# A fused Fourier filter and MLP: at least two MLP steps between one batch's spectrum units, and batch 1's units spread over more steps

## The chip, the core and the metric

The kernel runs on one core of a Trainium2 chip. TensorE (PE) multiplies matrices, loading weights (PEld) beside its matmuls; VectorE (DVE), ScalarE (ACT) and GpSimd (POOL) do elementwise work; SyncE (SP) and POOL queue DMA transfers. Matmuls write to PSUM, from which DVE and ACT evacuate to SBUF. The metric is the device time of one execution in microseconds, the median of several runs.

## The reference

Eight sequences of 3008 tokens with 256 channels are filtered in the frequency domain, and every token then goes through an MLP.

```python
X = np.fft.rfft(x, axis=1)                    # x: 8 x 3008 x 256
F = (filt_r + 1j * filt_i)[None, :, :]
y = np.fft.irfft(X * F, n=x.shape[1], axis=1)
h = y.reshape(24064, 256) @ w_in              # w_in: 256 x 2048
g = h * (1.0 / (1.0 + np.exp(-beta * h)))     # beta: one per hidden unit
out = g @ w_out                               # w_out: 2048 x 256
```

## The kernel before

The transform of length 3008 = 47 x 64 is done with small matrices in four stages. For each batch: stage 1 (`s1`, 16 units) multiplies x by a table of cosines and sines, stages 2 and 3 (`s23`, 15 units, the "spectrum units") multiply by a second table, by the filter, and by the inverse of the second table, and stage 4 (`s4`, 16 units) multiplies by the inverse of the first. Between the stages the data are turned round through scratch tiles in DRAM: `s1` stores to `d1` (line 621), `a2_read` loads from it (line 628), `s23` stores to `d2` (line 669), `zz_read` loads from it (line 676). Stage 4 leaves `y`, the MLP's input.

The MLP runs over 47 blocks of 512 tokens and, in each, over 16 slices of 128 hidden units: 752 **steps**. A step s emits two matmuls that make `hps` (line 825, 512 columns each), the ScalarE activation that makes `gT` of it (line 834), then whatever transform units the plan has for this step, and then four matmuls of 256 columns (line 867) that add step s - 2's `gT` into the block's output `acc`. In a block's first slice only two of these four are emitted, and six in the next one. At a block's last slice the two halves of `acc` are copied to `ost` (both on DVE, but one half on ACT in blocks 0 to 5) and stored (lines 786 to 800). That falls in steps with s mod 16 = 1.

Batch 0's transform is done ahead of the first step, up to some units that are planned as `uz`. The transform of batch b > 0 is laid between the MLP steps of batch b - 1, by a **plan** that is written out by hand: `plan[s]` is a list of units that step s emits, in order. `place(a, z, units, clear, per)` spreads a list evenly from step a to step z; a step takes at most `per` units, counting those already there, and the next free one is used where it is full; with `clear` a unit that falls in the first two or last two steps of a block is moved on to the third of the next. A batch b from 2 on starts at step a = `first_step[b - 1]` (80, 176, 272, ...): its spectrum units are spread from a + 3 to a + 47, `zz_read` is in a + 53, the next batch's `s1` from a + 48 to a + 61, and `s4` from a + 63 to a + 78. Batch 1 has its own numbers, because it shares steps 0 to 79 with the rest of batch 0.

A spectrum unit i of `s23` works on two of 24 frequencies, and emits in this order:

- two matmuls of 256 columns into `ps2` (line 638; traces show tiles without their number, so `ps`),
- three DVE operations that read `ps2`: `p_t` (line 649) and two halves of `q_t` (lines 650 and 653),
- one POOL addition that makes `v_t` (line 654),
- from i = 3 on, two matmuls of 256 columns with the `v_t` of unit i - 3 into `ps3` (line 664), and an ACT evacuation of it to `z` (line 107, called at 667). Units 12, 13 and 14 have this last part alone. Every third unit is followed by a store of `z` to `d2`.

All PSUM tiles of the transform (`ps1`, `ps2`, `ps3`, `ps4`, `pz`) share one pool of three buffers, `fpsum`. Which of the three a tile gets is decided when the program is built, and a tile's first matmul waits for the reader of the tile that had the buffer before. `hps` has two buffers and `acc` three. Each engine runs its instructions in order, so a matmul that waits holds up everything behind it on PE. SP's queue is in order too, and holds all stores and all DMAs between the stages; x is loaded from POOL's queue.

Of the kernel before, what the change touches and what calls it, by code (L numbers as in the profile page):

```python
# [37 lines left out]
def kernel(  # L38
# [450 lines left out]
    for i in range(NK // 2 + FLAG):  # L489
# [6 lines left out]
        if i in TAB:  # L496
            n = TAB.index(i)
# [101 lines left out]
    def start(b):  # L599
        d1 = dpool.tile([J, KP, D], BF16, name="d1", tag="d1")  # L600
        d2 = dpool.tile([J, KP, D], BF16, name="d2", tag="d2")
        st[b] = {
            "x": xs.pop(b),
            "d1r": d1.rearrange("j r d -> r j d"),
            "d2r": d2.rearrange("j r d -> r j d"),
            "d1c": d1.rearrange("j (a k) d -> (j a) k d", a=4),
            "d2c": d2.rearrange("j (a k) d -> (j a) k d", a=4),
        }

    def s1(b, i, on_act):  # L610
        s = st[b]
        g, jj = divmod(2 * i, JG)
        if jj == 0:
            s["a1"] = apool.tile([KP, JG, D], BF16, name="a1", tag="a1")
        ps = fpsum.tile([P, 512], F32, name="ps1", tag="f")
        nc.tensor.matmul(  # L616
            ps[:KP], lhsT=t1[:], rhs=s["x"][:, 2 * i : 2 * i + 2, :], start=True, stop=True
        )
        evac(s["a1"][:, jj : jj + 2, :], ps[:KP], on_act)
        if jj + 2 == JG:  # L620
            nc.sync.dma_start(s["d1r"][:, g * JG : (g + 1) * JG, :], s["a1"][:])

    def a2_read(b):
        s = st[b]
        s["a2"] = []
        for h in range(NG):
            t = a2pool.tile([P, KG, D], BF16, name="a2", tag="a2")
            nc.sync.dma_start(t[:], s["d1c"][:, h * KG : (h + 1) * KG, :])
            s["a2"].append(t)
# [41 lines left out]
    def zz_read(b):  # L671
        s = st[b]
        s["zz"] = []
        for h in range(NJG):
            t = zzpool.tile([KP, JG, D], BF16, name="zz", tag="zz")
            nc.sync.dma_start(t[:], s["d2r"][:, h * JG : (h + 1) * JG, :])
            s["zz"].append(t)
# [12 lines left out]

    plan = {}

    def place(a, z, units, clear=False, per=1):
        last_at = a
        for n, go in enumerate(units):
            at = a + (z - a) * n / max(1, len(units) - 1)
            at = max(int(at), last_at)
            if clear and (at % NFB < 2 or at % NFB > 13):
                at += (2 - at) % NFB
            while len(plan.get(at, ())) >= per:  # L700
                at += 1
            plan.setdefault(at, []).append(go)
            last_at = at
        return last_at

    def u1(b, act=False):
        def unit(i):
            def go():
                if i == 0:
                    start(b)  # L710
                s1(b, i, act and i % 2 == 1)

            return go

        return [unit(i) for i in range(J // 2)]

    def u23(b):
        return [lambda i=i: s23(b, i) for i in range(NK // 2 + VLAG)]

    def u4(b, act=False):  # L720
        return [lambda i=i: s4(b, i, act and i % 2 == 1) for i in range(J // 2)]

    def uz(g, act=False):
        return [lambda i=i: turn_z(g, i) for i in range(2)] + [
            lambda i=i: last_z(g, i, act) for i in range(2 * NDC)
        ]

    def uf(a, z):
        return [
            go  # L730
            for k0 in range(a, z, JG)
            for at in (0, M)
            for go in load_filter(frr, filt_r, at, k0, JG, nc.sync)
        ]


    def ut(n):
        return [
            lambda k=k: nc.vector.tensor_scalar_mul(
                t3[M:P, k : k + NK // n], t3b[M:P, k : k + NK // n], -1.0  # L740
            )
            for k in range(0, NK, NK // n)
        ]

    def ux(b):
        def go():
            xs[b] = load_x(b, X_WHOLE)

        return [go]

    place(2, 14, uz(1, True))
    place(15, 29, uz(2))
    units = uz(3, True)
    place(20, 24, units[:2], per=2)
    place(34, 58, units[2:])

    first_step = [(S * b // TB) * NFB for b in range(B + 1)]
    if B > 1:
        units = u1(1, True)
        place(3, 8, units[: J // 4], per=2)  # L760
        place(10, 10, uf(0, JG), per=9)
        at = place(9, 14, units[J // 4 :], per=9)
        place(at + 1, at + 1, [lambda: a2_read(1)] + uf(JG, NK), per=9)
        place(14, 20, ut(4), per=2)
        at = place(25, 56, u23(1), per=2)
        assert at < 60
        place(60, 60, [lambda: zz_read(1)], per=9)
        place(67, 79, u4(1), per=2)
    if B > 2:
        place(36, 36, ux(2), per=9)  # L770
        at = place(50, 66, u1(2, True), per=3)
        assert at < 74
        place(74, 74, [lambda: a2_read(2)], per=9)
    for b in range(2, B):
        a = first_step[b - 1]
        place(a + 3, a + 47, u23(b), True)
        place(a + 53, a + 53, [lambda b=b: zz_read(b)], per=9)
        if b + 1 < B:
            place(a + 6 if b == 2 else a - 8, NBLK * NFB, ux(b + 1), per=9)
            place(a + 48, a + 61, u1(b + 1))  # L780
            place(a + 68, a + 68, [lambda b=b: a2_read(b + 1)], per=9)
        place(a + 63, a + 78, u4(b))
# [29 lines left out]
    for s in range(len(steps) + LAG):  # L812
        if s < len(steps):
# [5 lines left out]
            while pos < t0 + tn:  # L819
                b, n0 = divmod(pos, S)  # L820
# [20 lines left out]
        if s >= LAG:  # L841
# [16 lines left out]
            per = acc[0].shape[1]  # L858
# [55 lines left out]
```

## Time and profile before

| | us |
|---|---|
| median of 3 runs | 785.22 (784.85 to 785.43) |
| the profiled execution's own time | 785.37 |
| its span, first to last instruction | 783.3 |
| PE busy | 768.8 |
| ACT busy | 594.4 |
| DVE busy | 393.3 |
| POOL busy | 144.4 |

The profile shows one execution, with times from the span's start. Ends of matmuls are modelled, their starts are not, so the pace of TensorE is read from starts. Step 0's first matmul is at 36.2 us. The granted TensorE clock is full speed in all slices. A number after "x" counts merged instructions, and square brackets give the idle time of an engine before an instruction and what ended it.

### The profile page before, as it was taken

What the parts mean: (1) busy time and instruction counts of PE and PEld (TensorE: products, weight loads), DVE (VectorE), ACT (ScalarE), POOL (GpSimd) and SP (SyncE); (2) the same over time, 40 slices, a digit from 0 to 9 for tenths busy, and PEclk for the clock granted to TensorE, in tenths of its full rate; (3) what the DMA queues carried; (4) which work ended last, traced back from release to release, by engine and by line L of the source; (5) the groups of instructions that cost most, each with busy time, mean ns of one, the idle gap of its engine ahead of it and who ended that gap; (6) DMA issues with size and microseconds to landing.
All of it is one profiled execution on the core that took longest, in us unless ns stands there. A gap on an engine that the chain in (4) does not pass through costs nothing.

```text
span 783.3 us, 15454 instructions
## 1 busy us (share of the span) xinstructions
PE 768.8 (98%) x6015; PEld 547.8 (70%) x6111; DVE 393.3 (50%) x645; ACT 594.4 (76%) x922; POOL 144.4 (18%) x143
## 2 busy tenths in 40 slices
PE   8899999999999999999999999999999999999997
PEld 5767667666776667866668666786667766776665
DVE  7848836646446563474635746267452761500101
ACT  6987887886678867787677876778767788677776
POOL 8522501320013100231002310024000330000000
PEclk9999999999999999999999999999999999999999
DMA  9979764517801186022850238412371114100101
GB/s 190 253 174 228 176 191 132 128 67 202 221 28 68 68 209 194 28 81 94 197 167 28 95 111 183 149 64 81 108 209 40 64 68 128 49 34 28 55 28 54
DMA packets 84185, 91.46 MB, mean 117 GB/s; under 512 B 4498, under 2 KB 74276, under 8 KB 83154
## 3 DMA queue, kind: packets, MB, share of 16 engines
q1 hardware_dynamic: 81008, 73.95, 30.8%
q0 software_dynamic: 2816, 16.26, 10.7%
q8 instruction: 48, 0.79, 0.4%
q10 hardware_dynamic: 288, 0.26, 0.1%
q14 instruction: 25, 0.20, 0.1%
HBM read 57.16 MB, written 46.66 MB: 133 GB/s over the span
## 4 chain that ended last, share of the span: by engine, by line
PE 96%; ACT 1%; issue 1%; DMA 1%; DVE 1%; POOL 0%; DVEq 0%; POOLq 0%
PE acc L867 43%; PE hps L825 39%; PE ps L616 3%; PE ps L541 3%; PE ps L664 3%; PE ps L638 2%; DMA xg<-in_x_dram 1%; PE psz L461 1%; PE pz L533 0%; PE psa L325 0%; ACT a L107 0%; DVE q_t L653 0%; DVE q_t L650 0%; PE pt L351 0%; PE ps L435 0%
## 5 line engine op out<-in xcount | busy, mean ns | idle before, releaser
L834 ACT ACTIVATE gT<-hps,beta_sb 128x512 bf16<-128x512 f32 x752 | 515.6, 687 | 176.5 <-PE hps L825 155.4
L867 PE MATMUL acc<-wout_sb,gT 128*128 128x256 bf16 x3008 | 451.4, 272 | 2.7
L825 PE MATMUL hps<-y,win_sb 128*128 128x512 bf16 (+8 forms) x1636 | 427.6, 350 | 0.4 <-ACT gT L834 0.3
L867 PEld LDWEIGHTS <-gT 128*128 128x128 bf16 x3008 | 285.6, 98 | 127.6 <-ACT gT L834 0.2
L825 PEld LDWEIGHTS <-win_sb 128*128 128x128 bf16 x1730 | 165.0, 98 | 24.7 <-issue 0.6
L654 POOL TENSOR_TENSOR v_t<-p_t,q_t 128x512 bf16<-128x512 f32 x84 | 106.6, 1269 | 390.4 <-DVE q_t L653 327.6
L109 DVE COPY ost<-acc 128x512 f32<-128x512 f32 (+1 forms) x88 | 56.2, 677 | 192.6 <-PE acc L867 189.6
L109 DVE CAST a<-ps 96x512 bf16<-96x512 f32 x96 | 65.9, 686 | 87.3 <-PE ps L616 86.8
L111 DVE TENSOR_SCALAR y<-ps 128x376 bf16<-128x376 f32 (+1 forms) x119 | 63.9, 544 | 61.3 <-PE ps L541 61.2
L649 DVE TENSOR_TENSOR p_t<-ps,frr 128x512 f32<-128x512 f32 x84 | 58.1, 692 | 31.3 <-PE ps L638 28.9
L653 DVE TENSOR_TENSOR q_t<-ps,fri 64x512 f32<-64x512 f32 x84 | 58.2, 693 | 1.2
L650 DVE SCALAR_TENSOR_TENSOR q_t<-ps,fri 64x512 f32<-64x512 f32 x84 | 57.4, 684 | 1.1
L541 PEld LDWEIGHTS <-zz 96*128 96x128 bf16 x512 | 35.3, 97 | 29.3 <-issue 0.5
L107 ACT ACTIVATE z<-ps 128x512 bf16<-128x512 f32 x84 | 49.5, 589 | 0.0
L616 PE MATMUL ps<-xg,t 94*96 94x512 bf16 x112 | 42.1, 381 | 0.7
L541 PE MATMUL ps<-t,zz 96*128 96x94 bf16 x448 | 36.7, 205 | 1.1
L664 PE MATMUL ps<-v_t,t 128*128 128x256 bf16 x168 | 32.2, 274 | 0.8 <-DVE q_t L653 0.3
L638 PE MATMUL ps<-a,t 128*128 128x256 bf16 x168 | 32.1, 273 | 0.4
L118 POOL DMA_DIRECT2D xg<-in_x_dram x22 | 12.1, 552 | 101.7 <-PE acc L867 97.6
L638 PEld LDWEIGHTS <-t 128*128 128x128 bf16 x168 | 15.8, 98 | 14.6
L664 PEld LDWEIGHTS <-t 128*128 128x128 bf16 x168 | 15.3, 98 | 10.8 <-ACT z L107 3.8
L616 PEld LDWEIGHTS <-t 94*96 94x96 bf16 x112 | 13.6, 123 | 11.8
(120 smaller groups left out, 195.0 us busy)
## 6 DMA issues: line engine op xcount, KB each, us to landing
out_dram<-ost SPq DMA_DIRECT2D x80, 256.0 KB, 2.1
d<-a SPq DMA_DIRECT2D x28, 384.0 KB, 3.4
a<-d SPq DMA_DIRECT2D x28, 384.0 KB, 4.4
d<-z SPq DMA_DIRECT2D x28, 384.0 KB, 2.3
zz<-d SPq DMA_DIRECT2D x28, 384.0 KB, 6.8
xg<-in_x_dram POOLq DMA_DIRECT2D x6, 1280.0 KB, 10.0
frr<-in_filt_r_dram SPq DMA_DIRECT2D x12, 256.0 KB, 7.5
out_dram<-ost SPq DMA_DIRECT2D x18, 128.0 KB, 2.5
```

What stands on the lines that cost most here:

```text
L109: nc.vector.tensor_copy(dst, src)
L111: nc.vector.tensor_scalar_mul(dst, src, scale)
L541: nc.tensor.matmul(ps[:, e, :NP], lhsT=zz[:, jj + e, dc * P : (dc + 1) * P], rhs=tab[:], start=True, stop=True,)
L616: nc.tensor.matmul(ps[:KP], lhsT=t1[:], rhs=s["x"][:, 2 * i : 2 * i + 2, :], start=True, stop=True)
L638: nc.tensor.matmul(ps[:, e, :], lhsT=t2[:, k0 + e, 3:5, :].rearrange("p c k -> p (c k)"), rhs=s["a2"][g][:, kk + e, :], start=True, stop=True,
L649: nc.vector.tensor_tensor(p_t[:], ps[:], frr[:, ks_, :], ALU.mult)
L653: nc.vector.tensor_tensor(q_t[:M], ps[M:P], fri[M:P, ks_, :], ALU.mult)
L654: nc.gpsimd.tensor_tensor(v_t[:], p_t[:], q_t[:], ALU.add)
L664: nc.tensor.matmul(ps[:, e, :], lhsT=t3[:, k0 + e, :], rhs=v_t[:, e, :], start=True, stop=True)
L825: nc.tensor.matmul(hps[:, pos - t0 : pos - t0 + ln], lhsT=win_sb[:, dc, fb * P : (fb + 1) * P], rhs=ys[b][:, dc, n0 : n0 + ln], start=(dc ...
L834: nc.scalar.activation(gT[:, :tn], hps[:, :tn], ACT.Silu, scale=beta_sb[:, fb : fb + 1])
L867: nc.tensor.matmul(acc[tb // per][:, tb % per, :], lhsT=g_[:, tb * P : (tb + 1) * P], rhs=wout_sb[:, f_, :], start=(f_ == 0 and tb % per = ...
```

## The change

`place` gets an argument `gap`: a unit is put at least `gap` steps behind the one before it of the same list. The spectrum units of all batches are placed with a gap of 2. Batch 1's are spread from step 25 to 58 instead of 56, the first stage of batch 2 from step 54 to 68 instead of 50 to 66, and batch 2's `a2_read` is in step 75 instead of 74.

```diff
-    def place(a, z, units, clear=False, per=1):
+    def place(a, z, units, clear=False, per=1, gap=0):
         last_at = a
         for n, go in enumerate(units):
             at = a + (z - a) * n / max(1, len(units) - 1)
-            at = max(int(at), last_at)
+            at = max(int(at), last_at + gap if n else last_at)
             if clear and (at % NFB < 2 or at % NFB > 13):
                 at += (2 - at) % NFB
             while len(plan.get(at, ())) >= per:
...
-        at = place(25, 56, u23(1), per=2)
+        at = place(25, 58, u23(1), per=2, gap=2)
         assert at < 60
         place(60, 60, [lambda: zz_read(1)], per=9)
         place(67, 79, u4(1), per=2)
     if B > 2:
         place(36, 36, ux(2), per=9)
-        at = place(50, 66, u1(2, True), per=3)
-        assert at < 74
-        place(74, 74, [lambda: a2_read(2)], per=9)
+        at = place(54, 68, u1(2, True), per=3)
+        assert at < 75
+        place(75, 75, [lambda: a2_read(2)], per=9)
     for b in range(2, B):
         a = first_step[b - 1]
-        place(a + 3, a + 47, u23(b), True)
+        place(a + 3, a + 47, u23(b), True, gap=2)
```

Worked through the plan, the spectrum units stand in these steps (for batches 2 to 7 counted from a):

```
batch 1 before  25 27 29 31 33 36 38 40 42 44 47 49 51 53 56
batch 1 after   25 27 29 32 34 36 39 41 43 46 48 50 53 55 58
batch b before   3  6  9 12 18 19 21 25 28 34 35 37 40 43 50
batch b after    3  6  9 12 18 20 22 25 28 34 36 38 40 43 50
```

Batch 2's 16 units of stage 1 move from steps 50 to 66 to steps 54 to 68: before, the last was in step 66; after, the last three are in 66, 67 and 68, the latter two behind units of batch 1's stage 4. Units of the other lists stay in their steps.

## Prediction

> **What bounds the kernel now.** I read the page's busy shares and chain first, then the waits, then the timeline at each wait of TensorE.
>
> ```profile
> PE 768.8 (98%) x6015; PEld 547.8 (70%) x6111; DVE 393.3 (50%) x645; ACT 594.4 (76%) x922; POOL 144.4 (18%) x143
> ...
> PE 96%; ACT 1%; issue 1%; DMA 1%; DVE 1%; POOL 0%; DVEq 0%; POOLq 0%
> ```
>
> TensorE (PE) is the bound: it holds 96% of the chain. Nothing that another engine gains counts unless PE waits less. So I looked for PE's own waits, weight loads included, in the waits:
>
> ```profile
> PEld L664 <- ACT z L107: 3.8, 12, 0.5
> ...
> PEld L664 <- DVE q_t L653: 1.2, 2, 0.6
> ...
> PE ps L541 <- DVE q_t L653: 0.5, 1, 0.5
> ```
>
> The columns are total us, times, longest. Twelve times the second pair of matmuls in a spectrum unit (L664) waited for ScalarE's evacuation of `z`: two for each of batches 2 to 7. The other three are in batch 1. The total of 3.8 counts the weight load's idle time, part of which lies beside the matmul before it, so I take what PE lost from starts. On this trace's PE timeline a 512-column matmul is 0.217 us after the one before, a 256-column one 0.109; a plain step is 2 x 0.217 + 4 x 0.109 = 0.87 us, a spectrum unit 4 x 0.109 = 0.436, a stage-1 unit 0.217, a stage-4 unit 0.165. What a start is late against this is lost. One such place, batch 3, timeline:
>
> ```profile
> 239.02 0.38 PE L638 MATMUL ps<-a,t 128*128 128x256 bf16 x2
> ...
> 239.86 0.59 ACT L107 ACTIVATE z<-ps 128x512 bf16<-128x512 f32 x1
> 239.89 0.69 DVE L649 TENSOR_TENSOR p_t<-ps,frr 128x512 f32<-128x512 f32 x1
> ...
> 240.10 0.38 PE L638 MATMUL ps<-a,t 128*128 128x256 bf16 x2
> ...
> 240.50 0.11 PEld L664 LDWEIGHTS <-t 128*128 128x128 bf16 x2 [0.30 <-ACT z L107]
> 240.51 0.39 PE L664 MATMUL ps<-v_t,t 128*128 128x256 bf16 x2
> ...
> 241.29 0.69 DVE L653 TENSOR_TENSOR q_t<-ps,fri 64x512 f32<-64x512 f32 x1
> ```
>
> Unit 4 (239.02) is in step a+18, unit 5 (240.10) in a+19. Unit 5's L664 should start 0.22 after its L638, at 240.32, and starts at 240.51: 0.18 us lost. In the built program its PSUM tile has the buffer of unit 4's `ps3`, and ACT had started on that at 239.86 and was done at 240.45, because `gT` of the same step goes first. Units 9 and 10 (a+34, a+35) do the same. Going through all gaps: 0.38 + 0.18 in batch 2 (in the first an `ost` copy on ACT is in the way too), 0.18 + 0.18 in each of batches 3 to 7. **That is 0.57 + 5 x 0.37 = 2.41 us.** Batch 1 lost 0.43 at 75.34 (step 34), 0.42 at 84.58 (step 42) and 0.29 at 94.40 (step 51), 1.14 us in all, each behind DVE's `q_t` (L653).
>
> **The change part by part.** It adds and removes no instruction; it moves them, and the loss goes where a wait is no longer late.
>
> *Batches 2 to 7.* Unit 5 goes from a+19 to a+20, 6 from a+21 to a+22, 10 from a+35 to a+36, 11 from a+37 to a+38. Unit 5's L664 would start 0.87 later than it should now, at 240.32 + 0.87 = 241.19; z of unit 4 ends at 240.45, so 0.74 us are to spare (in batch 2, where it ended 0.38 late, still 0.5). What is late next? DVE's three operations take 0.69 + 0.68 + 0.69, with gaps 2.12 us a unit, against 2 x 0.87 + 0.436 = 2.18 us for two steps with a unit: it keeps up, barely. Unit 4's last ends at 241.98 and unit 6's L638, which waits for it, comes at 240.97 + 2.18 = 243.15: 1.2 to spare. DVE is behind here (unit 5 starts at 242.01, when unit 4 is done), so units 5 and 6 end when they end now, and POOL's `v_t` with them; unit 7 and later stay put. Units 9 to 12 are two steps apart where 11 and 12 were three; unit 12's matmuls wait for unit 10's `q_t`, which ends 5.1 us after unit 9's L638, and they come after about 6.5. The store of `z` behind units 5 and 11 moves 0.9 us later on SP; the one that `zz_read` waits for is behind unit 14, which stays. Saved: all 2.41 us.
>
> *Batch 1.* Unit 3 goes to step 32, 4 to 34. The built program has unit 4's L664 wait for unit 3's `q_t`. DVE is still busy with unit 2 until 73.17 whether unit 3 comes in step 31 or 32, so unit 3's `q_t` ends at 73.19 + 2.10 = 75.29. Without a unit in step 31, L638 of unit 4 comes at 74.65 and L664 at 74.87: 0.47 lost, in place of the 0.43 there now. Where a unit's L664 waits for the `q_t` of the unit two steps before (steps 43 and 50, each with a stage-4 unit between), it comes 2.18 + 0.165 + 0.218 = 2.56 after that unit's L638, and `q_t` is done after 0.22 + 0.27 (matmul end to DVE, as from 154.32 to 154.81 in batch 2) + 2.12 + 0.05 = 2.66: 0.1 each. The three-step gaps ahead (36 to 39, 43 to 46) let DVE catch up, which is why the 0.42 and 0.29 shrink to this.
>
> *Batch 2's stage 1.* Units 13, 14, 15 now fall in steps 66 to 68, beside stage 4. Unit 14's matmul waits for ACT's evacuation of unit 13. From the end of `hps` in step 66 its natural start is 0.217 + 0.218 (a block's first slice has half of L867) + 0.434 + 2 x 0.165 = 1.20. ACT starts `gT` after 0.26 to 0.3, the evacuation 0.58 behind that, and this takes 0.59, then 0.06: 1.5 to 1.6. Lost: 0.34, new. Moving `a2_read` costs nothing: its loads wait for the last `d1` store, which waits on SP behind eight output stores (4.49 us of issuing from 112.20 before), as it does now; they started at 120.09 with their first use at 129.11, 9 us cover against a landing of 5.2. If that cover went, each us beyond would be a us of PE at step 83.
>
> Batch 1 after: 0.47 + 0.1 + 0.1 + 0.34 = 1.0 against 1.14. **Sum: 2.41 + 0.15 = 2.6 us less**, 785.37 - 2.6 = 782.8 for the profiled execution, which is 0.15 above the median of the runs: 782.6.
>
> *A rule that speaks against the change.* Step 58 now has `gT`, a stage-4 evacuation, unit 14's `z` and a stage-1 evacuation on ACT, and 53, 55, 60 have two or three. The row first:
>
> ```profile
> 94.49 0.72 ACT L834 ACTIVATE gT<-hps,beta_sb 128x512 bf16<-128x512 f32 x1
> 95.06 0.64 ACT L107 ACTIVATE z<-ps 128x512 bf16<-128x512 f32 x1
> 95.53 0.62 ACT L107 ACTIVATE a<-ps 96x512 bf16<-96x512 f32 x1
> ```
>
> Starts lie 0.57 and 0.47 apart, closer than the durations: they overlap. The Trainium skill, "ScalarE: Activation LUTs", section "Rules for kernel authors", budgets about 0.3 us per activation and 0.83 ns per element, 0.725 us for 512. By the row, steps 58 to 60 hold 0.58 + 0.38 + 2 x 0.48, 0.58 and 0.58 + 0.48 = 3.6 us of ACT against 3.65 of PE (1.47 + 1.09 + 1.09): no loss. By the rule it is 2.8 + 0.7 + 1.45 = 4.95, 1.3 over; `hps` with two buffers lends 0.44, so 0.9 would be lost, and some 0.5 more at step 67: a saving of 1.2. I take the row, as the engine itself shows it; the rule's end stays in the range.
>
> **The rivals.**
>
> *DVE takes over the wait.* At two steps it has 0.06 us spare, and one `ost` copy is 0.68. If in batches 2 to 7 the 12 places keep 0.1 each as in batch 1, 1.2 of 2.41 is lost: 783.8. For it: batch 1's waits are all DVE's. Against it: there the buffers in question hang on ACT's `z`, as the waits show. Bound: 12 x 0.18, nothing gained, 785.0.
>
> *ACT piles up*, as the rule has it: 784.0.
>
> *Slower: batch 1's `zz_read` comes too late for step 67.* Unit 14 moves from step 56 to 58, stage 4 stays in 67. Before:
>
> ```profile
> 102.02 0.34 SPq L669 DMA_DIRECT2D d<-z  x1
> ...
> 104.36 3.63 SPq L676 DMA_DIRECT2D zz<-d  x4
> ```
>
> L664 of unit 14 was at 100.56, the store at 102.02, the reads at 104.36, and by the semaphore's updates in the trace the first read was in at 109.02, 4.66 later; PE needed it at 112.48. After, the store comes 1.7 behind L664 (ACT has one more ahead), the first read is in at 1.7 + 2.3 + 4.7 = 8.7; step 67's first use comes after 0.22 + 0.22 + 0.44 + 8 x 0.87 + 8 x 0.217 - 0.22 + 0.43 = 9.8. So 1.1 us to spare, 3.5 now. A read that took the slowest landing of these reads anywhere, 7.9, would stop PE for 2.1: 784.7. The time gets worse than before from a landing of 4.66 + 1.1 + 2.6 = 8.4 us; at 10.4 it would be 787.2. Against it: none took that long, and stores stand behind these reads on SP, not ahead.
>
> *The change doesn't do what it says:* the order of instructions shows units 5, 6, 10 and 11 moved in every batch, so only a different choice of buffers could keep the waits, and the built program has none in batches 2 to 7 on a reader less than two steps old. Then 785.2.
>
> **How the numbers follow.** About 0.2% (1.6 us) is what a measurement of this kernel can tell from no change: faster is below 783.65. The forecast, 782.6 with 782.0 to 783.3 for its own terms (0.3 for what batch 1 keeps or sheds, 0.3 between runs), has 0.78. DVE 0.08 and ACT 0.08 lie around 783.8 and 784.0, a third of each faster; late reads 0.04, of which 0.03 slower; no effect 0.02. Faster 0.78 + 0.05 = 0.83, slower 0.03, the rest 0.14. The range 781.8 to 784.2 takes in DVE's and ACT's cases and leaves out the late reads.
>
> **What would show it.** In the profile after, `PEld L664 <- ACT z` should be down from 12 times to at most one; unit 5 of batch 3 should start L664 0.22 behind its L638. Around 75 us an L664 should wait about 0.5 for `q_t`, and near 111 an L616 about 0.3 for ACT's `a`. An L541 waiting for a DMA there means the reads are late; `hps` waiting for `gT` between 95 and 105 means ACT piles up; L664 or L638 waiting for `q_t` in batches 2 to 7 means DVE. A time above 784.2 would make the forecast wrong, and so would a gain with the twelve waits still there.

## The result, and the profile after

The changed kernel takes 783.06 us, the median of 6 runs (782.44 to 783.57), against 785.04 (784.7 to 785.71) for the kernel before in the same measurement: a ratio of 0.9973 with a 95% interval of 0.996 to 0.9986. It is faster by 0.27%.

On the page after, the first lines of busy time and of the chain hardly differ from before:

```profile
span 781.3 us, 15549 instructions
...
PE 771.6 (99%) x6111; PEld 548.4 (70%) x6111; DVE 392.9 (50%) x645; ACT 594.3 (76%) x922; POOL 144.3 (18%) x143
...
PE 95%; DVE 2%; ACT 1%; DMA 1%; issue 0%; POOL 0%; DVEq 0%; POOLq 0%
```

PE's busy time even grows, as 96 matmul records are missing from the trace before (6015 against 6111). Busy time is no measure here. The waits show what changed (total us, times, longest):

```profile
PEld L664 <- DVE q_t L653: 1.4, 3, 0.6
...
DVE ost L109 <- DMA out_dram<-ost: 1.1, 1, 1.1
...
PE ps L664 <- DVE q_t L653: 0.7, 2, 0.4
```

The line `PEld L664 <- ACT z L107`, twelve times before, is gone. What is left of L664's waits are three in batch 1, all for DVE, and there is a line that was not there before: a copy of `ost` on DVE waited 1.1 us for an output store to land. Batch 3's units 4 and 5 in the timeline after:

```profile
238.95 0.38 PE L638 MATMUL ps<-a,t 128*128 128x256 bf16 x2
...
239.80 0.59 ACT L107 ACTIVATE z<-ps 128x512 bf16<-128x512 f32 x1
...
241.13 0.38 PE L638 MATMUL ps<-a,t 128*128 128x256 bf16 x2
...
241.34 0.38 PE L664 MATMUL ps<-v_t,t 128*128 128x256 bf16 x2
```

ACT's `z` of unit 4 is done at 239.80 + 0.59 = 240.39, and unit 5's L664 starts at 241.34, 0.21 behind its L638, as two 256-column matmuls take. Nothing is lost, and 0.95 us would have been to spare. (The prediction worked out 0.74: it took step a+19 as 0.87 us long, but that is a block's second slice, with six matmuls of L867 in place of four, 1.09 us.)

To compare kernels by their profiles I use the stretch from the first to the last matmul of `hps`, because what lies ahead of it is the same code and varied between executions. Before, then after (the view of the tile `hps`; min/median/max ns, then first and last start in us):

```profile
L825 PE MATMUL hps<-y,win_sb x1636: 192/379/380, 36.2 to 777.6; 128*128 128x512 bf16 x132, 128*128 128x448 bf16 x8, 128*128 128x384 bf16 x8, 128*128 128x320 bf16 x8
```

```profile
L825 PE MATMUL hps<-y,win_sb x1730: 192/379/380, 36.6 to 775.6; 128*128 128x512 bf16 x142, 128*128 128x448 bf16 x8, 128*128 128x192 bf16 x8, 128*128 128x64 bf16 x7
```

741.4 us became 739.0, 2.4 less. The medians differ by 2.0 alone. Medians of few runs are blunt here: the 20 runs of the kernel before that stand beside the first experiments lie in two groups, 9 at 784.6 to 784.9 and 11 at 785.4 to 786.3, so a median moves with their mix. The table has the stretch for every kernel, read from the timelines to 0.01 us, and what PE lost in batch 1, read from starts as in the prediction (each start against the nominal distance from the one before; what is late by less than 0.06 us is left out):

| kernel | median us | before beside it | ratio, 95% interval | stretch us | L664 waits for z | lost in batch 1, us |
|---|---|---|---|---|---|---|
| before | 785.04 | | | 741.39 | 12 | 0.43 + 0.42 + 0.29 = 1.14 |
| after | 783.06 | 785.04 | 0.9973 (0.996 to 0.9986) | 739.00 | 0 | 0.47 + 0.53 + 0.06 + 0.28 = 1.34 |
| gap from batch 2 alone | 783.17 | 785.46 | 0.9966 (0.9952 to 0.9979) | 738.85 | 0 | 0.43 + 0.43 + 0.09 + 0.21 = 1.16 |
| batch 1's edits alone | 785.61 | 785.46 | 1.0 (0.9991 to 1.0009) | 741.10 | 12 | 0.48 + 0.08 + 0.06 + 0.27 = 0.89 |
| first gap only | 783.57 | 785.46 | 0.9979 (0.997 to 0.9988) | 740.03 | 6 | 0.43 + 0.43 + 0.25 = 1.11 |
| after, four `ost` | 782.55 | 785.06 | 0.9965 (0.9952 to 0.9978) | 738.65 | 0 | 0.48 + 0.18 + 0.07 + 0.28 = 1.01 |
| after, stage 1 to 66 | 782.98 | 785.06 | 0.9972 (0.9962 to 0.9983) | 738.62 | 0 | 0.48 + 0.25 + 0.06 + 0.17 = 0.96 |
| after, replanned | 782.33 | 785.06 | 0.9967 (0.9955 to 0.998) | 738.66 | 0 | 0.11 + 0.88 = 0.99 |
| replanned, four `ost` | 781.9 | 785.06 | 0.9957 (0.9945 to 0.997) | 737.77 | 0 | 0.12 |

Where did the 2.4 us come from? Each matmul of L867 stands in both programs in the same order, so its start, counted from the first `hps`, can be compared between the two traces. At step 80, when batch 1 is through, the changed kernel is 0.15 us behind; at the end it is 2.39 ahead. So batches 2 to 7 gained 2.54 us, and batch 1 lost 0.15. Each of the twelve places gained 0.195 us (the first one 0.39), 0.01 more than the late start itself, because the second matmul of a late pair comes 0.119 us behind the first (240.51 to 240.63 in batch 3) and not 0.109.

### The profile page after: what moved, and what is told of

The parts are those of the page before. It is cut to its first block, busy times and chain, and to the rows that moved or that the text cites. A ratio compares the mean times of both kernels' runs of the same rounds, so it can differ in the third digit from the quotient of the medians.

```text
span 781.3 us, 15549 instructions
## 1 busy us (share of the span) xinstructions
PE 771.6 (99%) x6111; PEld 548.4 (70%) x6111; DVE 392.9 (50%) x645; ACT 594.3 (76%) x922; POOL 144.3 (18%) x143
## 4 chain that ended last, share of the span: by engine, by line
PE 95%; DVE 2%; ACT 1%; DMA 1%; issue 0%; POOL 0%; DVEq 0%; POOLq 0%
PE acc L867 42%; PE hps L825 41%; PE ps L616 3%; PE ps L541 3%; PE ps L664 2%; PE ps L638 2%; DMA xg<-in_x_dram 1%; PE psz L461 0%; ACT a L107 0%; DVE q_t L650 0%; PE pz L533 0%; DVE q_t L653 0%; PE psa L325 0%; PE pw L187 0%; DVE p_t L649 0%
## 5 line engine op out<-in xcount | busy, mean ns | idle before, releaser
L867 PE MATMUL acc<-wout_sb,gT 128*128 128x256 bf16 x3008 | 451.3, 272 | 0.0
L825 PE MATMUL hps<-y,win_sb 128*128 128x512 bf16 (+8 forms) x1730 | 447.7, 351 | 0.3 <-ACT gT L834 0.3
L867 PEld LDWEIGHTS <-gT 128*128 128x128 bf16 x3008 | 285.6, 98 | 128.2 <-ACT gT L834 0.2
L541 PEld LDWEIGHTS <-zz 96*128 96x128 bf16 x512 | 35.3, 97 | 28.9
L107 ACT ACTIVATE z<-ps 128x512 bf16<-128x512 f32 x84 | 49.5, 589 | 0.2 <-PE ps L664 0.2
L616 PE MATMUL ps<-xg,t 94*96 94x512 bf16 x112 | 41.9, 381 | 0.1
L541 PE MATMUL ps<-t,zz 96*128 96x94 bf16 x448 | 36.7, 204 | 0.0
L664 PE MATMUL ps<-v_t,t 128*128 128x256 bf16 x168 | 32.1, 273 | 0.7 <-DVE q_t L653 0.7
L638 PE MATMUL ps<-a,t 128*128 128x256 bf16 x168 | 32.1, 273 | 0.0
L638 PEld LDWEIGHTS <-t 128*128 128x128 bf16 x168 | 15.8, 98 | 14.4
L616 PEld LDWEIGHTS <-t 94*96 94x96 bf16 x112 | 13.6, 123 | 11.9
L664 PEld LDWEIGHTS <-t 128*128 128x128 bf16 x168 | 16.1, 98 | 7.5 <-DVE q_t L653 1.4
```

The source lines that it names most:

```text
L541: nc.tensor.matmul(ps[:, e, :NP], lhsT=zz[:, jj + e, dc * P : (dc + 1) * P], rhs=tab[:], start=True, stop=True,)
L616: nc.tensor.matmul(ps[:KP], lhsT=t1[:], rhs=s["x"][:, 2 * i : 2 * i + 2, :], start=True, stop=True)
L638: nc.tensor.matmul(ps[:, e, :], lhsT=t2[:, k0 + e, 3:5, :].rearrange("p c k -> p (c k)"), rhs=s["a2"][g][:, kk + e, :], start=True, stop=True,
L664: nc.tensor.matmul(ps[:, e, :], lhsT=t3[:, k0 + e, :], rhs=v_t[:, e, :], start=True, stop=True)
L825: nc.tensor.matmul(hps[:, pos - t0 : pos - t0 + ln], lhsT=win_sb[:, dc, fb * P : (fb + 1) * P], rhs=ys[b][:, dc, n0 : n0 + ln], start=(dc ...
L867: nc.tensor.matmul(acc[tb // per][:, tb % per, :], lhsT=g_[:, tb * P : (tb + 1) * P], rhs=wout_sb[:, f_, :], start=(f_ == 0 and tb % per = ...
```

## The experiments

**Which part of the change is the gain?** The gap without batch 1's numbers, and batch 1's numbers without the gap:

```diff
 # the kernel before, with place() as changed
-        place(a + 3, a + 47, u23(b), True)
+        place(a + 3, a + 47, u23(b), True, gap=2)
```

> The kernel before, with the gap of two steps for batches 2 to 7 only; batch 1 and batch 2's stage 1 stay as before. Theory (the gain is the twelve waits of L664 for ACT's z in batches 2 to 7, and batch 1's edits are worth nothing or a small loss): the twelve waits are gone, batch 1 keeps its losses of 0.43, 0.42 and 0.29 at steps 34, 42 and 51, the time is 2.4 us under before's, at or a little under that of the change as a whole. Rival (a good part comes from spreading batch 1): under 1.5 us gained, and the change as a whole is clearly faster than this.

```diff
 # the kernel after
-        place(a + 3, a + 47, u23(b), True, gap=2)
+        place(a + 3, a + 47, u23(b), True)
```

> The kernel after, without the gap for batches 2 to 7: batch 1's and batch 2's stage 1's edits alone. Theory: the twelve waits of L664 for ACT's z are back, batch 1 loses 1.34 us as in the changed kernel's profile (0.47, 0.53, 0.06, 0.28) instead of 1.14, so the time is before's plus 0.2 us, no change that can be measured. Rival (spreading batch 1 helps): 0.5 us or more under before.

With the gap alone the twelve waits are gone and the time is 783.17 us, as that of the whole change; the stretch is 738.85, 2.54 us under before's, with batch 1 as it was. Batch 1's edits alone leave it at 741.10, the time at 785.61, and this line in the waits, the same as before the change:

```profile
PEld L664 <- ACT z L107: 3.8, 12, 0.5
```

So all of the gain that can be seen in the times comes from batches 2 to 7, and spreading batch 1 gives or takes a few tenths: 0.15 lost in the changed kernel's profile, 0.29 gained in this one. The theory's size for batch 1 was off, though: it expected the 1.34 us of the changed kernel's profile, and the run lost 0.89. The difference is step 43: 0.08 here, 0.53 there, with the same plan for batch 1. That part of the loss differs between executions of one and the same program.

**Is each wait a loss of its own?** The gap only between the first eight units:

```diff
 # the kernel with the gap from batch 2 alone
-            at = max(int(at), last_at + gap if n else last_at)
+            at = max(int(at), last_at + gap if 0 < n < 8 else last_at)
```

> The kernel before, with the gap only between the first eight units of batches 2 to 7: unit 5 goes to a+20 and 6 to a+22, while units 10 and 11 stay at a+35 and a+37. Theory (each wait is a loss of its own): six of the twelve waits remain, all at a+35, 0.38 + 5 x 0.18 = 1.3 us gained. Rival (the loss is shifted, so that a place that is left makes up for the one taken away, or both must go before anything is gained): the second wait grows to some 0.37 and nothing is gained, or the whole 2.4 us.

```profile
PEld L664 <- ACT z L107: 1.8, 6, 0.3
```

Six waits remain, and each start is as late as it was: 0.185 us in all six batches. The stretch is 740.03, 1.36 us under before's, and the six places that were cleared account for it: 0.39 + 5 x 0.195 = 1.37. The medians differ by 1.9 us, with an interval from 0.9 to 2.4, which does not contradict it; eight of the ten runs lie at 783.4 to 783.8, and from the lower group of before's runs (median 784.84) to these (783.49) it is 1.35. These stalls of PE add up: a late start delays all that follows, and nothing in these traces makes it up again.

**What is the 0.53 us at step 43?** The changed kernel's timeline of DVE shows where it begins:

```profile
74.96 0.69 DVE L653 TENSOR_TENSOR q_t<-ps,fri 64x512 f32<-64x512 f32 x1
76.74 0.69 DVE L109 COPY ost<-acc 128x512 f32<-128x512 f32 x1 [1.08 <-DMA out_dram<-ost]
77.46 0.69 DVE L649 TENSOR_TENSOR p_t<-ps,frr 128x512 f32<-128x512 f32 x1
```

The `ost` copy of step 33 takes a buffer whose store has not landed, and DVE stands for 1.08 us. Before the change unit 4 was in step 33, and since a step emits its planned units ahead of the output copies, unit 4's products stood ahead of this copy (they started at 75.32, the copy came at 77.45 and found its buffer free). Moved to step 34, they stand behind it. From there DVE is 1 us late, at two steps a unit it has 0.06 us each to catch up, and at step 43 L664 waits for `q_t`. If that is so, a fourth buffer must remove it. (To make room, `a2` got four buffers instead of five.)

```diff
 # the kernel after
-    a2pool = pool("a2pool", 5)
+    a2pool = pool("a2pool", 4)
...
-    ostp = pool("ostp", 3)
+    ostp = pool("ostp", 4)
```

> The kernel after, with four instead of three ost buffers, and four instead of five a2 buffers to make room for them. It leaves nothing out. Theory (in the changed kernel's profiled execution unit 4's products stood on DVE behind the ost copy of step 33, which waited 1.08 us for an earlier output store to land, and this made the 0.53 us at step 43): with a fourth buffer no ost copy waits for a DMA near 76 us in any execution, and step 43 loses 0.1 to 0.2 instead of 0.53; the others (0.47 at 34, about 0.3 at 67) stay. Time 0.1 to 0.4 us under after's. Rival (the 0.53 is DVE's backlog from steps 25 to 34, and the store has no part in it): 0.5 stays at step 43.

The copy starts at 75.03 without a wait, and steps 42 and 43 lose 0.18 (at an L541, a stage-4 matmul) instead of 0.53; 0.48 at step 34 and 0.28 at step 67 stay. But this run alone does not prove it: batch 1's edits alone, with three buffers, had no such wait either, and the new buffers also changed which PSUM tile shares a buffer with which (the L541 of step 42 waits for another engine's semaphore than in the changed kernel). What follows settles it.

**What is the 0.28 us at step 67?** Stage 1 of batch 2 (its matmul is L616) now ends in step 66:

```diff
 # the kernel after
-        at = place(54, 68, u1(2, True), per=3)
+        at = place(54, 66, u1(2, True), per=3)
```

> The kernel after, with batch 2's stage 1 spread from step 54 to 66 instead of 68, so that no unit of it stands beside stage 4 in steps 67 and 68. Theory (the 0.28 us that L616 loses at step 67 is ACT's evacuation of the unit of step 66): no L616 waits at step 67; ACT is fuller before, and a step near 59 may lose up to 0.2 to an L616. Time 0.1 to 0.3 us under after's. Rival (the loss at step 67 is the landing of the first zz read): an L541 waits there instead, 0.3 us.

Nothing waits at step 67 now, no L541 either, so the zz reads were not late, and the 0.28 went with stage 1's units. In the changed kernel ACT's evacuation of the unit before is what ends last there:

```profile
112.27 0.58 ACT L107 ACTIVATE a<-ps 96x512 bf16<-96x512 f32 x1
...
112.91 0.38 PE L616 MATMUL ps<-xg,t 94*96 94x512 bf16 x1
```

0.17 us comes back where it was expected, at the L616 that starts at 103.84. The time, 782.98, is not to be told from the changed kernel's. Step 43 lost 0.25 in this run, behind this copy of step 33:

```profile
76.37 0.69 DVE L109 COPY ost<-acc 128x512 f32<-128x512 f32 x1 [0.79 <-ACT y L107]
```

The profile puts this wait down to ACT, but by the semaphore's updates in the trace it was the store again: its last part landed at 76.25, and the copy started 0.12 us later, as in the changed kernel (76.62 and 76.74). That gives three executions of one program, because this kernel, the changed one and batch 1's edits alone do not differ before step 54: the copy waited 0.79, 1.08 and 0 us, and step 43 lost 0.25, 0.53 and 0.08. The 0.29 us between the two waits is found again as 0.28 on PE.

**Can batch 1's losses be planned away?** Three places of the plan are changed, aimed at DVE's backlog (two stage-4 evacuations before unit 3) and at step 67:

```diff
 # the kernel after
-    place(15, 29, uz(2))
+    place(15, 29, uz(2, True))
...
-        at = place(25, 58, u23(1), per=2, gap=2)
+        at = place(25, 57, u23(1), per=2, gap=2)
...
-        at = place(54, 68, u1(2, True), per=3)
+        at = place(54, 66, u1(2, True), per=3)
```

> The kernel after, with three numbers of its plan changed: batch 0's third stage-4 group is evacuated by ACT instead of DVE, batch 1's spectrum units end in step 57 instead of 58, batch 2's stage 1 in step 66 instead of 68. Theory (batch 1's losses at 34, 43 and 67 are DVE's backlog, which starts with the two stage-4 evacuations in steps 26 and 29, and ACT's at step 67): 0.2 to 0.4 us lost in batch 1 instead of 1.34 or 0.90; time 0.5 to 1 us under after's, 3 us under before's. If the ost copy of step 33 waits for its store, up to 0.5 comes back at step 43. Rival (DVE's pace of two steps a unit is the cause, not its backlog): 0.5 at step 34 stays.

> The same plan as in the run before it, with four ost and four a2 buffers. Theory: no ost copy waits near 76 us, batch 1 loses 0.2 to 0.4 us in every execution; at most 0.4 us under the one with three ost buffers, or equal to it if that one's profile shows no such wait. Rival (the fifth a2 buffer matters): an L638 waits for a load near step 83 or in the first unit of a later batch, and the time is higher.

The second has the same plan, and four buffers of `ost` and `a2`; up to step 43 the transform's matmuls wait for the same engines' semaphores in both. With three buffers the losses at steps 34 and 67 are gone, but the copy of step 33 waited longer than in any other run, and L664 at step 43 lost 0.88 (0.11 more at step 42):

```profile
75.90 0.69 DVE L109 COPY ost<-acc 128x512 f32<-128x512 f32 x1 [2.22 <-DMA out_dram<-ost]
76.62 0.69 DVE L649 TENSOR_TENSOR p_t<-ps,frr 128x512 f32<-128x512 f32 x1
```

With four:

```profile
74.76 0.69 DVE L109 COPY ost<-acc 128x512 f32<-128x512 f32 x1
75.64 0.69 DVE L649 TENSOR_TENSOR p_t<-ps,frr 128x512 f32<-128x512 f32 x1 [0.18 <-DMA out_dram<-ost]
```

No copy waits (the 0.18 in front of `p_t`, which reads no `ost`, is a wait for the unit's L638: `p_t` starts 0.48 us after it, as from 154.32 to 154.81 in the prediction), and batch 1 loses 0.12 us in all, less than the 0.2 to 0.4 expected. The stretch is 737.77, 0.9 us under that with three buffers and 1.2 under the changed kernel's. So the wait for the store is what step 43 lost. The expectations of "up to 0.5" for it, and of "at most 0.4 us" between the two, were too small, since the wait came to 2.22 us this time. The fifth `a2` buffer was not missed: no L638 waits for a load. DVE's pace of 2.12 us a unit against 2.18 for two steps is enough once there is no backlog; that rival is out. At 781.9 us, 0.43% under the kernel before (0.9945 to 0.997), this version has the lowest time of the study; its interval overlaps that of the change, so that it is faster than the change rests on the stretch and the waits.

## Why the prediction was right

- *What bounds it.* PE, and its own waits alone: the stretch between first and last `hps` became 2.39 us shorter, where 2.6 was forecast. The profiled execution's own time shows 2.0 (785.37 to 783.37), because its first `hps` came at 36.6 instead of 36.2; over nine profiles that start lay between 35.7 and 36.8, in the same code.
- *Batches 2 to 7.* The mechanism is as forecast: none of the twelve waits is left, the DVE chain starts and ends as worked out (unit 5's products still follow directly on unit 4's), and the gap alone gives the whole gain. The size is 2.54 us against 2.41, as a late pair also cost the 0.01 between its matmuls.
- *Batch 1, step 34.* 0.47 us forecast, 0.47 measured: `q_t` of the unit before, on a DVE that was still busy.
- *Batch 1, steps 43 and 50.* 0.1 each forecast. Step 50 lost 0.06. Step 43 lost 0.53: this is the term that was mis-sized. "The three-step gaps ahead (36 to 39, 43 to 46) let DVE catch up" counted DVE's work and not its queue. Moving unit 4 from step 33 to 34 put it behind an output copy that may wait for a store, and none of the prediction's bounds held a wait that before it stood behind the unit. Where the store lands in time, step 43 loses the 0.1 forecast (0.08 in batch 1's edits alone).
- *Step 67.* 0.34 us forecast, 0.28 measured, and the experiment that takes stage 1 out of the step removes it.
- *Batch 1's sum.* 1.0 forecast, 1.34 in this execution, 0.89 in another: a loss of 0.15 us against before in the one and a gain of 0.29 in the other, where a gain of 0.15 was forecast. With the 2.54, the whole gain is 2.4 us as measured, and an estimated 2.8 where the store is in time, instead of a steady 2.6. That the forecast lies inside this is in part luck: the one term was too small by 0.13 us, the other too favourable by 0.3.
- *ACT.* Taking the distance between starts was right: no `hps` waits for `gT` around steps 53 to 60, nor is anything lost there, though ACT has four activations in step 58. The 0.725 us for 512 elements, an estimate from the Trainium skill ("ScalarE: Activation LUTs", section "Rules for kernel authors"), is a budget for one activation, and near the 0.69 that `gT` lasts in this trace. The prediction's rival added it up as if activations did not overlap, and that would have cost about 0.9 us there.
- *DVE as a rival.* It took nothing in batches 2 to 7: no L664 or L638 is late there. (The bound given for it, 12 x 0.18 us, would leave 0.4 of the 2.6 and comes to 784.8, not 785.0.)
- *The slower rival.* The zz reads were issued at 106.51, the first was in at 110.04 by the semaphore's updates, 3.5 us later, and was needed at 112.30: 2.3 us to spare, where 1.1 was worked out with 4.7 for the landing. Moving `a2_read` cost nothing, as forecast: issued at 120.79, first needed at 129.63, and no L638 waited. (Before the change five output stores stood ahead of it on SP, not eight: `112.20 4.49 SPq L800 DMA_DIRECT2D out_dram<-ost  x5`.)

## What to carry to other kernels

Where one in-order engine bounds a kernel, list its own waits, read from starts of instructions what each one costs, and move the waiter by more than the wait: these losses add up and each comes back whole. When a unit is moved by a step, look on every engine's queue at what it is moved past; an instruction that was harmless behind it, such as an output copy that waits for a store's buffer, is in its way when it stands ahead. A plan that leaves an engine 0.06 us per unit to catch up turns one late microsecond into a loss many steps on.

## What the runs showed of the hardware

Consecutive activations on ScalarE start closer together than they last. Where they follow directly in the changed kernel's trace, the next one starts 0.57 to 0.67 us after a `gT` (the median is 0.585), which the profile shows as 0.69, and mostly 0.48 to 0.50 after a `z`, shown as 0.59. Adding up durations overstates its load by about a sixth to a quarter.

When one and the same output store has landed differs between executions enough to change what a queue waits for: in three executions of the same code the copy of step 33 waited 1.08, 0.79 and 0 us for it, and a single profile would have given any of these as the cost. The store itself was not slower: from issue to landing its last part took 7.6, 8.1 and 8.0 us. What differed was when SP came to issue it, 32.4, 31.6 and 30.9 us after step 0's first matmul. SP held it back each time until 0.01 or 0.02 us after the landing of a filter load eight places ahead in its queue, which uses the same semaphore. Why that load landed at different times is not shown.
